# One issue line for the first loads: joint Wq/Wk quarters on SP, and eight first projections over eight PSUM banks

## The chip, the cores and the metric

The kernel runs on one core of a Trainium2 chip. The metric is the device time of one execution in microseconds (us). Engines are named as in the profile: PE (matmul), PEld (its weight loads), DVE (vector), ACT (scalar), POOL, SP (which only issues transfers). ACTq and SPq are the rows in which ACT and SP issue transfers.

## What is computed

The reference mixes two branches over x (2048 tokens of 512 values, bf16) with a gate per token:

```
g = sigmoid((x * gate_w).sum(-1))
qkv = x @ wqkv                                  # 512 x 1536: q, k, v of 32 heads with 16 values
logits[s, w] = q[s] . k[s - 2 w] / 4,  w = 0..7   # masked before the first token
a = (softmax(logits) applied to v[s - 2 w]) @ wo
b = (gelu(layernorm(x)^T @ w1 + b1) @ w2 + b2)^T
out = g * a + (1 - g) * b
```

## The kernel before

All work is registered as operations of a small planner in the kernel (`_Sched`, L48 to L271). An operation has an engine, an estimated duration, what it reads and writes, and a priority. `_pass` (L145) plays the list through with these estimates and so fixes one order for each engine; `plan_waits` (L234) then gives every instruction the semaphore waits that it needs. For a transfer, `lands` can state a due time at which the planner is to take it for finished; it changes the planned order and nothing else. Two chains written out by hand fix the order on DVE (L957) and of part of ACT.

The part that matters here is the start. Q and K are computed transposed: a projection (`f_proj`, L612) is four matmuls of 128x128 weights on 512 tokens, one for each 128 rows ("quarter", 0 to 3) of wqkv, added up in one PSUM bank. Its rhs is `XT`, x transposed. Sixteen-value heads are split over four interleaved column sets, so Q of one block of 512 tokens takes four projections (q0 to q3), and K four (k0 to k3).

For block 0, XT comes in two ways. Its quarter 0 is loaded plainly (`d_xp`, 128 columns of x for 512 tokens, rows of 256 B), transposed on PE (`f_tr`, L540, instructions on L544) and copied out of PSUM by ACT (`ev_tra`, L553) and DVE (`ev_trb`, L555). Quarters 1 to 3 are written transposed by a transposing transfer (`ld_xt0`, L470, issued on L473). Blocks 1 to 3 come by transposing transfers of all four quarters (`ld_xt`, L457, issued on L460). Plain x for the layernorm comes by `ld_x` (L439), weights by `ld_w` (L447). All plain transfers are issued on L429. PE runs matmuls on a constant (`f_warm`, L532, instructions on L536) until the first data are there.

Order of the first issues before the change:

- ACT: `d_xp` (128 KB), then quarter 0 of Wq (128 KB).
- SP: block 0's transposing transfer (384 KB), quarters 1, 2, 3 of Wq (128 KB each), quarters 0-1 and 2-3 of Wk (256 KB each), x tiles 0-1 (256 KB), block 1's transposing transfer (512 KB), x tiles 2-3, x tiles 4-7, blocks 2 and 3, x tiles 8-11 and 12-15, Wv, and then the weights of the later stages. From x tiles 2-3 on, each issue waits for an earlier transfer to have landed (`throttle`, L433: the fifth before it in `init_dmas`).

The first eight projections (L633) run in groups: q0 to q3 with quarter 0 into banks 0 to 3, then the same four with quarter 1, 2 and 3, then k0 to k3 with quarters 0-1 into banks 4 to 7, then k0 to k3 with quarters 2-3. That is 4 + 4 + 4 + 4 + 8 + 8 = 32 matmuls. ACT copies each finished bank to SBUF (L625 for Q, L628 for K and V). After them PE runs the projections of the other blocks in banks 0 to 3 (`seq_proj`, L643), first the eight of block 1.

On DVE the order from the start is: L424, `ev_trb`, layernorm statistics of x tiles 0 to 3 (`ln1`, L572), then the first two products of Q and shifted K (`qkm`, L688), which need Q and K of blocks 0 and 1. Reductions of these products on PE (`qkr`, L696) free the product buffers. Later come the softmax (L742 to L775), the weighted sum of V (L795 to L800) and the mix (`cmb`, L897). PE goes on with the first and second layer of the token branch (L810, L860) and the output projection (L876).

Of the kernel before, what the change touches and what calls it, by code (L numbers as in the profile page):

```python
# [13 lines left out]
D = 512  # L14
# [319 lines left out]
def bass_gated_mix__sliding_local_dilated__mixer_token_mlp__prompt_kernel(nc, A_x, A_wqkv, A_wo, B_x, B_w1, B_b1, B_w2, B_b2, gate_w, out, dbg=None):  # L334
    with contextlib.ExitStack() as es:
# [3 lines left out]
        sch = _Sched()  # L339

        x2d = A_x[0]
        xv = x2d.rearrange("(t p) d -> p t d", p=128)
        wqkv_v = A_wqkv.rearrange("(dt p) c -> p dt c", p=128)
# [7 lines left out]
        WQKV = view("WQKV", BF16, [(3 * D, 4), (1, 3 * D)])  # L351
# [63 lines left out]
        A = sch.add  # L415
# [12 lines left out]
        def mk_dma(dst, src):  # L428
            return lambda e: e.dma_start(dst, src)  # L429

        init_dmas = []
# [4 lines left out]
        def prev_dma():  # L436
            return [init_dmas[-1]] if init_dmas else []

        def ld_x(t0, n, q="sp"):  # L439
            ds = sch.dsem("x%d" % t0)  # L440
            op = sch.dma(q, mk_dma(X[:, t0:t0 + n, :], xv[:, t0:t0 + n, :]), n * 128 * D * 2, ds,
                         writes=["x%d" % t for t in range(t0, t0 + n)], deps=throttle() if q == "sp" else [], after=prev_dma() if q == "sp" else [], name="d_x%d" % t0)
            if q == "sp":
                init_dmas.append(op)
            return op

        def ld_w(tn, d0, n, q="sp"):  # L447
            ds = sch.dsem("wqkv%d_%d" % (tn, d0))
            op = sch.dma(q, mk_dma(WQKV[:, d0:d0 + n, tn * D:(tn + 1) * D], wqkv_v[:, d0:d0 + n, tn * D:(tn + 1) * D]),
                         n * 128 * D * 2, ds, writes=["wqkv%d_%d" % (tn, dt) for dt in range(d0, d0 + n)],  # L450
                         deps=throttle() if q == "sp" and n == 4 else [], after=prev_dma() if q == "sp" else [],
                         issue=0.65 if n == 4 else 0.45, name="d_wp%d_%d" % (tn, d0))
            if q == "sp":
                init_dmas.append(op)
            return op
# [14 lines left out]
        def ld_xt0():  # L470
            ds = sch.dsem("xt0")
            dst = XT[:, 1:4, 0:512]
            op = sch.dma("sp", lambda e: e.dma_start_transpose(dst, x2d[0:512, 128:512]), 512 * 384 * 2, ds, issue=1.25,  # L473
                         writes=XT0[1:4], after=prev_dma(), name="d_xt0")
            init_dmas.append(op)
            return op

        XP = view("OUTS", BF16, [(128, 4), (1, 128)])
        d_xp = sch.dma("act", mk_dma(XP, xv[:, 0:4, 0:128]), 512 * 128 * 2, sch.dsem("xp"), writes=["outs0"], issue=0.4, name="d_xp")

        first_loads = [ld_w(0, 0, 1, "act"), ld_xt0(), ld_w(0, 1, 1), ld_w(0, 2, 1), ld_w(0, 3, 1), ld_w(1, 0, 2), ld_w(1, 2, 2),
                       ld_x(0, 2)]
        ld_xt(1)
        first_loads.append(init_dmas[-1])
        for op_, t_ in zip(first_loads, (3.4, 4.6, 5.0, 5.4, 5.8, 6.6, 7.4, 8.2, 10.6)):
            op_.lands = t_
            op_.deps.clear()
        d_xp.lands = 3.1
        first_loads[0].order.add(d_xp)
        init_dmas[:] = [first_loads[1]] + first_loads[5:]  # L490
        ld_x(2, 2)
        ld_x(4, 4)
        ld_xt(2)
# [6 lines left out]
        def ld_w1(j):  # L500
# [4 lines left out]
            if j < 4:  # L505
# [8 lines left out]
                       writes=["wo"], deps=throttle(), after=prev_dma(), name="d_wo")  # L514
# [4 lines left out]
        for i_, (v_, n_) in enumerate(((B_b1, NFT), (B_b2, NST))):  # L519
# [6 lines left out]
          writes=["btc"], name="t_b")  # L526
# [5 lines left out]
        def f_warm(n, w_=D):  # L532
            def fn(e):
                ins = None
                for _ in range(n):
                    ins = e.matmul(ps[:, 7, 0:w_], lhsT=CONE[:, 0:128], rhs=CONE[:, 0:w_], start=True, stop=True)  # L536
                return ins
            return fn

        def f_tr(h):  # L540
# [8 lines left out]
        w2_ = A("pe", f_warm(1, 256), 0.2, writes=["lg7_0", "lg7_1"], name="warm2", prio=-100)  # L549
        ta_ = A("pe", f_tr(0), 0.215, reads=["outs0", "ident"], writes=["lg5_0", "lg5_1"], after=[w2_], name="tr0", prio=-100)  # L550
        tr_ = A("pe", f_tr(1), 0.215, reads=["outs0", "ident"], writes=["lg6_0", "lg6_1"], after=[ta_], name="tr1", prio=-100)
        w3_ = A("pe", f_warm(1), 0.43, writes=["lg7_0", "lg7_1"], after=[tr_], name="warm3", prio=-100)
        A("act", lambda e: e.activation(out=XT[:, 0, 0:256], in_=ps[:, 5, 0:256], func=AF.Copy), 0.35, reads=["lg5_0", "lg5_1"],  # L553
          writes=["xt0_0"], name="ev_tra", prio=0)
        A("dve", lambda e: e.tensor_copy(out=XT[:, 0, 256:512], in_=ps[:, 6, 0:256]), 0.35, reads=["lg6_0", "lg6_1"],  # L555
# [74 lines left out]
        tnames = ["q", "k", "v"]  # L630
        first = [(tn, dl) for tn in range(2) for dl in range(4)]
        fbn = [["acc%d" % b] for b in range(4)] + [["lg%d_0" % b, "lg%d_1" % b] for b in range(4, 8)]
        for (b0, d0, d1, s0, s1) in ((0, 0, 1, 0, 512), (0, 1, 2, 0, 512), (0, 2, 3, 0, 512), (0, 3, 4, 0, 512), (4, 0, 2, 0, 512), (4, 2, 4, 0, 512)):  # L633
            for b in range(b0, b0 + 4):
                tn, dl = first[b]
                last_main[0] = A("pe", f_proj(tn, dl, 0, b, d0, d1, s0, s1), 0.216 * (d1 - d0) * (s1 - s0) / 512,
                                 reads=xt_of(0, d0, d1) + ["wqkv%d_%d" % (tn, dt) for dt in range(d0, d1)],
                                 writes=fbn[b], after=[last_main[0]], name="pf_%s%d_%d_%d" % (tnames[tn], dl, d0, s0))
                last_main[0].order.add(w3_)
# [411 lines left out]
```

## Time and profile before

| | |
|---|---|
| time, median of 3 runs | 168.57 us (168.3 to 168.81) |
| the profiled execution: own time | 168.55 us |
| its span, first to last instruction | 167.3 us |
| PE busy | 162.1 us (97%) |
| DVE busy | 151.3 us (90%) |
| ACT busy | 75.1 us (45%) |
| granted TensorE clock, mean | 1.000 |
| transfers | 29.64 MB, mean 177 GB/s |

Starts are in us from the start of the span. A chain of waits is followed back from the last instruction: each piece is what the next one waited for. "x8" means eight instructions in one row; a row can hold many that run back to back. The profile shows a matmul of 512 columns as 379 ns long, though a new one starts every 0.2156 us when nothing is waited for, since matmuls overlap. For a transfer the profile gives when its engine issued it, how long the issue took, and how long after the start of the issue the data had landed.

### The profile page before, as it was taken

The numbers are of one execution on the slowest core, as the hardware profiler recorded it, in microseconds if no ns is written. First come the engines' busy times: TensorE is split into PE (matmuls) and PEld (weight loads), VectorE is DVE, ScalarE is ACT, GpSimd is POOL, SyncE is SP. The second block draws the span as 40 slices with busy tenths as digits, with TensorE's granted clock in tenths as the row PEclk, the third lists the DMA queues.
The fourth block names the chain that finished last, engine by engine and source line by source line (L and its number), as shares of the span: only waits on it lengthen the run. The fifth ranks groups of instructions, "written<-read, shape, count | busy, mean of one in ns | idle before, by whom it ended". The sixth has DMA issues, their size and how long they took to land.

```text
span 167.3 us, 2136 instructions
## 1 busy us (share of the span) xinstructions
PE 162.1 (97%) x845; PEld 77.5 (46%) x859; DVE 151.3 (90%) x154; ACT 75.1 (45%) x116; POOL 0.7 (0%) x8
## 2 busy tenths in 40 slices
PE   7699999999999999999999999999999999999994
PEld 2355555554454444444444444444444444444463
DVE  1055999999999999999999999999999999999896
ACT  3077688889899818793131121131231321310100
POOL 1000000000000000000000000000000000000000
PEclk9999999999999999999999999999999999999999
DMA  5999999959003846996779926462672570000454
GB/s 135 327 268 216 314 316 290 303 165 308 2 0 97 311 116 179 307 290 155 181 189 340 339 76 142 113 187 71 181 218 83 138 223 0 0 0 0 157 190 159
DMA packets 47625, 29.64 MB, mean 177 GB/s; under 512 B 9856, under 2 KB 46464, under 8 KB 47616
## 3 DMA queue, kind: packets, MB, share of 16 engines
q1 hardware_dynamic: 45120, 24.85, 54.4%
q10 hardware_dynamic: 2496, 4.66, 10.2%
q8 instruction: 7, 0.11, 0.3%
q14 instruction: 2, 0.02, 0.0%
HBM read 21.24 MB, written 2.10 MB: 140 GB/s over the span
## 4 chain that ended last, share of the span: by engine, by line
PE 91%; DMA 3%; DVE 2%; ACT 2%; issue 1%; ACTq 0%
PE ps L860 29%; PE ps L810 29%; PE ps L617 23%; PE ps L876 6%; PE ps L696 4%; DMA arena<-in_A_wqkv_dram 3%; DVE arena L897 2%; ACT L585 1%; ACT arena L628 1%; ACTq L429 0%; ACT arena L585 0%
## 5 line engine op out<-in xcount | busy, mean ns | idle before, releaser
L860 PE MATMUL ps<-arena 128*128 128x512 bf16 x220 | 48.5, 379 | 0.2
L810 PE MATMUL ps<-arena 128*128 128x512 bf16 x219 | 48.2, 379 | 0.4 <-issue 0.2
L617 PE MATMUL ps<-arena 128*128 128x512 bf16 x188 | 41.4, 379 | 1.6 <-DMA arena<-in_A_wqkv_dram 1.3
L688 DVE TENSOR_TENSOR arena<-arena 128x4096 bf16<-128x4096 bf16 (+1 forms) x12 | 35.5, 2998 | 2.5 <-ACT arena L628 2.1
L795 DVE TENSOR_TENSOR arena<-arena 128x8192 bf16<-128x8192 bf16 x8 | 35.0, 4419 | 0.0
L860 PEld LDWEIGHTS ps<-arena 128*128 128x128 bf16 x224 | 21.9, 98 | 26.4
L810 PEld LDWEIGHTS ps<-arena 128*128 128x128 bf16 x224 | 21.8, 98 | 26.6 <-ACT arena L726 0.4
L617 PEld LDWEIGHTS ps<-arena 128*128 128x128 bf16 x192 | 21.6, 113 | 21.5 <-issue 1.8
L928 ACT ACTIVATE arena<-ps,arena 128x512 bf16<-128x512 f32 x16 | 12.5, 778 | 39.4 <-PE ps L860 39.4
L798 DVE TENSOR_TENSOR arena<-arena 128x4096 bf16<-128x4096 bf16 (+1 forms) x16 | 27.0, 1751 | 0.0
L628 ACT ACTIVATE arena<-ps 128x512 bf16<-128x512 f32 x32 | 18.6, 596 | 4.5 <-PE ps L617 4.5
L831 ACT ACTIVATE arena<-ps,arena 128x512 bf16<-128x512 f32 x14 | 9.6, 687 | 22.2 <-PE ps L810 16.6
L572 DVE BATCH_NORM_STATS2 arena<-arena 128x6 f32<-128x512 bf16 x16 | 10.0, 682 | 6.1 <-DMA arena<-in_A_x_dram 6.1
L876 PE MATMUL ps<-arena 128*128 128x512 bf16 (+1 forms) x79 | 14.1, 336 | 0.1
L897 DVE SCALAR_TENSOR_TENSOR arena<-ps,arena 128x512 bf16<-128x512 f32 (+1 forms) x20 | 11.5, 637 | 0.9 <-PE ps L876 0.7
L596 ACT ACTIVATE arena<-arena 128x512 bf16<-128x512 bf16 x16 | 12.2, 804 | 0.0
L625 ACT ACTIVATE arena<-ps 128x512 bf16<-128x512 f32 x16 | 9.0, 597 | 6.2 <-PE ps L617 6.1
L876 PEld LDWEIGHTS ps<-arena 128*128 128x128 bf16 x80 | 7.8, 98 | 6.2
L672 DVE SCALAR_TENSOR_TENSOR arena<-arena 128x512 bf16<-128x512 bf16 x16 | 10.1, 689 | 0.0
L742 DVE TENSOR_TENSOR arena<-arena 128x512 bf16<-128x512 bf16 (+4 forms) x11 | 7.3, 667 | 0.6 <-ACT arena L761 0.2
L696 PE MATMUL ps<-arena 128*32 128x512 bf16 x128 | 7.3, 380 | 0.0
L726 ACT ACTIVATE arena<-ps 128x512 bf16<-128x512 f32 x8 | 4.7, 592 | 4.6 <-PE ps L696 4.6
(42 smaller groups left out, 40.0 us busy)
## 6 DMA issues: line engine op xcount, KB each, us to landing
arena<-in_B_w_dram SPq DMA_DIRECT2D x7, 1024.0 KB, 8.5
arena<-in_B_w_dram SPq DMA_DIRECT2D x8, 896.0 KB, 5.2
arena<-arena ACTq DMA_DIRECT2D x32, 128.0 KB, 2.9
arena<-in_A_x_dram SPq DMA_DIRECT2D x4, 512.0 KB, 6.1
out_dram<-arena SPq DMA_DIRECT2D x14, 128.0 KB, 1.7
arena<-in_A_x_dram SPq DMA_DIRECT2D x1, 1536.0 KB, 7.9
arena<-in_A_wqkv_dram SPq DMA_DIRECT2D x2, 256.0 KB, 3.8
arena<-in_A_x_dram SPq DMA_DIRECT2D x2, 256.0 KB, 3.6
```

The costliest lines, as they stand in the source:

```text
L596: A("act", (lambda t_: (lambda e: e.activation(out=X[:, t_, :], in_=X[:, t_, :], func=AF.Identity, scale=col(RSTD, t_), bias=col(NMR, t_)) ...
L617: ins = e.matmul(ps[:, bank, s0:s1], lhsT=lhsT, rhs=XT[:, dt, sb * 512 + s0:sb * 512 + s1], start=(dt == 0 and s0 == 0), stop=(dt == 3))
L628: return lambda e: e.activation(out=dst, in_=ps[:, bank, :], func=AF.Copy)
L688: return lambda e: e.tensor_tensor(out=PBL[buf][:, :, 512 * c0:512 * (c0 + nc_)], in0=in0, in1=in1, op=ALU.mult)
L696: ins = e.matmul(ps[32 * c:32 * c + 32, 4 + wl, :], lhsT=RP, rhs=PBL[buf][:, wl, c * 512:(c + 1) * 512], start=(dl == 0), stop=(dl == 3), ...
L795: A("dve", (lambda o_, i0, i1: (lambda e: e.tensor_tensor(out=o_, in0=i0, in1=i1, op=ALU.mult)))(pv, in0, in1), 4.4, reads=v_res + ["atx_% ...
L798: A("dve", (lambda pv_, n__: (lambda e: e.tensor_tensor(out=pv_[:, 0:n__], in0=pv_[:, 0:n__], in1=pv_[:, n__:2 * n__], op=ALU.add)))(pv, n ...
L810: ins = e.matmul(ps[:, bank, :], lhsT=W1W[:, slot, st, 128 * e_:128 * e_ + 128], rhs=X[:, st, :], start=(st == 0), stop=(st == NST - 1))
L860: ins = e.matmul(ps[:, bank, :], lhsT=W2S[slot][:, ft, 128 * e_:128 * e_ + 128], rhs=UT[:, ft, :], start=(ft == 0), stop=(ft == NFT - 1))
L876: ins = e.matmul(ps[:, bank, 0:c1 - c0], lhsT=OT[:, t, 128 * i:128 * i + 128], rhs=WO[:, t, c0:c1], start=(t == 0), stop=(t == 3))
L897: A("dve", (lambda i_, b_, c0_, c1_: (lambda e: e.scalar_tensor_tensor(out=T1[:, i_, c0_:c1_], in0=ps[:, b_, 0:c1_ - c0_], scalar=col(G, i ...
L928: A("act", (lambda i_, bank_: (lambda e: e.activation(out=T1[:, i_, :], in_=ps[:, bank_, :], func=AF.Identity, scale=col(OMG, i_), bias=co ...
```

## The change

The first loads are all issued on SP, in one line: `d_xp`, quarter 0 of Wq and Wk together (256 KB, rows of 2 KB), block 0's transposing transfer, quarters 1, 2 and 3 of Wq and Wk together (256 KB each), block 1's transposing transfer, x tiles 0-1. Then the line goes on as before. The due times for the planner are new. The first projections run in groups over all eight banks: q0 to q3 and k0 to k3 with quarter 0, the same eight with quarter 1, then q0 to q3 with quarter 2 and with quarter 3, then k0 to k3 with quarters 2-3 (8 + 8 + 4 + 4 + 8 = 32 matmuls). One more matmul on a constant, of 256 columns, stands ahead of them.

```diff
-        d_xp = sch.dma("act", mk_dma(XP, xv[:, 0:4, 0:128]), 512 * 128 * 2, sch.dsem("xp"), writes=["outs0"], issue=0.4, name="d_xp")
-
-        first_loads = [ld_w(0, 0, 1, "act"), ld_xt0(), ld_w(0, 1, 1), ld_w(0, 2, 1), ld_w(0, 3, 1), ld_w(1, 0, 2), ld_w(1, 2, 2),
-                       ld_x(0, 2)]
+        d_xp = sch.dma("sp", mk_dma(XP, xv[:, 0:4, 0:128]), 512 * 128 * 2, sch.dsem("xp"), writes=["outs0"], issue=0.4, name="d_xp")
+
+        def ld_qk(d):
+            ds = sch.dsem("wqk%d" % d)
+            op = sch.dma("sp", mk_dma(WQKV[:, d, 0:2 * D], wqkv_v[:, d, 0:2 * D]), 2 * 128 * D * 2, ds,
+                         writes=["wqkv0_%d" % d, "wqkv1_%d" % d], after=prev_dma(), issue=0.45, name="d_wqk%d" % d)
+            init_dmas.append(op)
+            return op
+
+        first_loads = [ld_qk(0), ld_xt0(), ld_qk(1), ld_qk(2), ld_qk(3)]
         ld_xt(1)
         first_loads.append(init_dmas[-1])
-        for op_, t_ in zip(first_loads, (3.4, 4.6, 5.0, 5.4, 5.8, 6.6, 7.4, 8.2, 10.6)):
+        first_loads.append(ld_x(0, 2))
+        for op_, t_ in zip(first_loads, (3.9, 5.3, 6.1, 6.8, 7.5, 9.6, 10.4)):
             op_.lands = t_
             op_.deps.clear()
         d_xp.lands = 3.1
         first_loads[0].order.add(d_xp)
-        init_dmas[:] = [first_loads[1]] + first_loads[5:]
+        init_dmas[:] = [first_loads[1]] + first_loads[3:]
...
-        w3_ = A("pe", f_warm(1), 0.43, writes=["lg7_0", "lg7_1"], after=[tr_], name="warm3", prio=-100)
+        A("pe", f_warm(1), 0.43, writes=["lg7_0", "lg7_1"], after=[tr_], name="warm3", prio=-100)
+        w3_ = A("pe", f_warm(1, 256), 0.2, writes=["lg7_0", "lg7_1"], after=[tr_], name="warm4", prio=-100)
...
-        for (b0, d0, d1, s0, s1) in ((0, 0, 1, 0, 512), (0, 1, 2, 0, 512), (0, 2, 3, 0, 512), (0, 3, 4, 0, 512), (4, 0, 2, 0, 512), (4, 2, 4, 0, 512)):
-            for b in range(b0, b0 + 4):
+        for (b0, nb, d0, d1, s0, s1) in ((0, 8, 0, 1, 0, 512), (0, 8, 1, 2, 0, 512), (0, 4, 2, 3, 0, 512), (0, 4, 3, 4, 0, 512),
+                                         (4, 4, 2, 4, 0, 512)):
+            for b in range(b0, b0 + nb):
```

In the order that the planner makes of it, PE and DVE keep their order but for these first groups. On ACT the two issues go, the copies of the first banks come in the order q0, q1, q2, k0, q3, k1, k2, q0 of block 1, k0 of block 1, k3, and a few later copies trade places with a neighbour. Block 2's transposing transfer now waits for quarter 3 of Wq/Wk, block 3's for block 1's, and x tiles 8-11 for x tiles 0-1.

## Prediction

> **What bounds the kernel now.** I read the chain of waits first, in order of time:
>
> ```profile
> 0.80 0.46 ACTq L429
> 1.25 0.03 issue
> 1.28 4.24 DMA arena<-in_A_wqkv_dram
> 5.52 0.09 issue
> 5.61 8.36 PE ps L617 x38
> ...
> 154.72 6.92 PE ps L876 x32
> 161.64 0.02 issue
> 161.67 3.98 DVE arena L897 x9
> ```
>
> The kernel waits 5.6 us for quarter 0 of Wq (issued by ACT at 1.28, landed 4.24 later); from then on PE runs to the end. Whatever moves PE's first projection moves the end, if no new wait appears. Next, the timeline of the start (start, length, engine and line):
>
> ```profile
> 0.80 1.35 SPq L473 DMA_TRANSPOSE arena<-in_A_x_dram  x1
> ...
> 2.22 2.49 SPq L429 DMA_DIRECT2D arena<-in_A_wqkv_dram  x5
> 3.30 0.34 PEld L544 LDWEIGHTS ps<-arena 128*128 128x128 bf16 x4 [0.66 <-issue]
> ...
> 3.96 0.42 DVE L555 CAST arena<-ps 128x256 bf16<-128x256 f32 x1 [2.45 <-PE ps L544]
> 4.75 0.47 SPq L429 DMA_DIRECT2D arena<-in_A_x_dram  x1
> 5.27 3.36 SPq L460 DMA_TRANSPOSE arena<-in_A_x_dram  x1
> 5.58 14.39 PEld L617 LDWEIGHTS ps<-arena 128*128 128x128 bf16 x68 [1.82 <-issue]
> 5.61 14.62 PE L617 MATMUL ps<-arena 128*128 128x512 bf16 x66 [1.26 <-DMA arena<-in_A_wqkv_dram]
> ```
>
> XT's quarter 0 is ready at 4.38, when the cast on L555 ends. PE has nothing to do until 5.61, and then starts a matmul every 0.2156 us. Last, the transfers in half microseconds (last two columns: busy share, GB/s):
>
> ```profile
> 2.00:2.50 0.50, 0.50 (x2) 0.15 (x1) 0.00 (x0) 0.50 (x1) 0.00 (x0) 1.00 0.67 153
> 2.50:3.00 0.50, 0.50 (x3) 0.15 (x1) 0.00 (x0) 0.50 (x1) 0.00 (x0) 1.00 1.28 287
> ...
> 5.50:6.00 0.50, 0.39 (x2) 0.26 (x3) 0.00 (x0) 0.00 (x0) 0.00 (x0) 1.00 1.00 316
> ...
> 8.00:8.50 0.50, 0.50 (x4) 0.29 (x3) 0.00 (x0) 0.00 (x0) 0.00 (x0) 1.00 1.62 231
> ```
>
> From 2 us on they are never idle: order, not latency, decides when a byte arrives.
>
> **The change, part by part.** Sizes in thousands of bytes: d_xp 131, a single Wq quarter 131, a joint quarter 262, block 0's transposing transfer 393, block 1's 524.
>
> *Start of the first group.* It needs the joint quarter 0 and XT's quarter 0. SP issues d_xp at 0.80 (0.46 long, as ACT's row) and the joint quarter at 1.28; the transposing transfer now comes behind it. Data flow from about 2.0; 393 have moved by about 3.6 by the windows (77 by 2.5, 220 by 3.0, 364 by 3.5), and the distance from moved to landed is 0.9 to 1.0 below: 4.5. So the group starts at 4.5 in place of 5.61, and 8 matmuls take 1.72: to 6.2. A start up to 0.4 later costs nothing, as the next wait is later. The added 256-column matmul (its twin before the data took 0.42) ends before 4.5: nothing.
>
> *Second group: the new limit.* It needs quarters 1 of XT and of the weights. By the line, 131+262+393+262 = 1048 must have moved. Before the change exactly as much had to be moved for Wq's quarter 3 (131+131+393+3x131), issued at 3.29 and landed 3.3 later, at 6.6. Summing the windows, 1048 are moved at 5.66, so 0.94 passes from moved to landed. A second way: transposing alone ran slower than the rest (about 520 of block 1 between 8.0 and 10.2: 245 GB/s, where plain loads ran at 316 to 354). Then 2.1 + 131 at 220 GB/s + 262 at 340 + 393 at 245 + 262 at 340 ends at 5.84, landing 6.8. The bounds from rows of issue to landing: issue of quarter 1 at 3.25 (0.80 + 0.46 + 0.5 + 1.35 and gaps), plus 3.3, the shortest of the wqkv rows, is 6.55; plus 4.2, the longest, is 7.45. I take 6.7.
>
> *The rest of the first 32.* 24 matmuls follow without a break: 6.7 + 24 x 0.2156 = 11.87. Before: 5.61 + 32 x 0.2156 = 12.51. Gain 0.64. Quarter 2 is due at 8.42 and quarter 3 at 9.29; as many bytes (1310 and 1573, the two Wk transfers) had landed before at 7.45 and 8.2 (issue 3.75 and 4.24, plus 3.7 and 4.0), so both are in time.
>
> *Block 1 and x tiles 0-1 change places.* Block 1, at 2097 bytes of the line, lies between x tiles 0-1 (1835, landed 4.1 after 4.75: 8.85) and its old place (2359, landed 5.5 after 5.27: 10.8): about 9.9, needed at 11.87. SP issues it at about 4.7 and, by the 3.36 row, is held by it to about 8, so x tiles 0-1 are issued at 8.0 and land at about 11 (the transfer that followed block 1 before took 3.0), x tiles 2-3 at 11.7 as before. The four statistics on DVE (1.29 for two) then end at about 13.5 in place of 13.02. The products they precede wait for K of block 1 anyway: 15.07 before, 2.56 after the first 32 matmuls, so 14.43 now. Nothing lost; the cover ends if x tiles 2-3 land 0.9 later than that.
>
> *Behind it.* Blocks 2 and 3 were issued at 9.81 and 13.62 and land at 15.8 and 18.3; they are needed 8 and 9 projections (0.8624 each) after the first 32: 18.8 and 19.6. Their changed waits point at transfers landed by 10. ACT loses two issues and has the same copies; copied banks are reused 3.4 us later, and a copy takes 0.60. DVE is dense too (90%), but at 42.15 it waits for PE's reductions, and these start on PE 1.2 after DVE's last product (37.36 to 38.58); near the end it waits again 0.72 for the output projection. So up to about 1.2 of PE's gain passes through.
>
> *Sum.* The profiled execution took 168.55 (span 167.3 and 1.25 around it), practically the median 168.57. 168.55 - 0.64 = **167.9**.
>
> *A rule against it.* In the first half microsecond of transfers, with d_xp and the transposing transfer flowing, only 153 GB/s were moved. The Trainium skill ("DMA: Bandwidth & Descriptors", Specifications) asks for at least 512 B per piece for line rate; d_xp has rows of 256 B, and now all the rest queues behind it. The traces before, with two queues, can't show that alone. What it would do is the second rival.
>
> **The rivals.**
>
> *No second wait* (gain 1.1): the transposing transfer and quarter 1 are there by 6.2. Then 4.5 + 32 x 0.2156 = 11.4, 167.4. For: landing of quarter 1 was 0.3 behind the transposing transfer's (6.0 and 5.7). Against: 1048 bytes by 5.3 means 320 GB/s from the first moment, and the first windows show 153 and 287.
>
> *d_xp holds the line.* Before, its slow pieces ran beside another queue's; now nothing runs beside them. If its 131 flow at the 153 of the first window (0.86) in place of 220 (0.60), and the transposing transfer starts late by as much again, everything behind is 0.4 later: second group at 7.1, end at 12.27, gain 0.24, 168.3. The rule above names this.
>
> *The transposing transfer takes its time from its issue: slower.* It landed 4.9, 5.5, 6.0 and 4.7 after issue in the four cases seen. It is now issued at 1.83 in place of 0.80. If 5.5 to 6.0 hold, it lands at 7.3 to 7.8 and quarter 1 0.3 behind: second group at about 7.9, end 13.07, 169.1. The price begins where the second group starts after 12.51 - 24 x 0.2156 = 7.34. For: the issue moves back a full microsecond, and it no longer runs beside another queue, where the busy share was 1.27. Against: the 5.5 and 6.0 were behind about 900 of other bytes; 393 stand ahead here, mostly gone at 3.2.
>
> *Gained, then lost:* x tiles 2-3 or block 3 slip by over a microsecond (SP held longer by block 1) and PE waits there: about 168.5.
>
> **How the numbers follow.** Forecast (second group between 6.3 and 7.0) 0.50; no second wait 0.12; d_xp 0.15; transposing transfer late 0.15; lost later 0.08. A measurement can tell about 0.3%, 0.5 us. Faster by more than that needs the second group before 6.85: most of the forecast, 0.38, and the 0.12: 0.50. Slower: the late transposing transfer, beyond its threshold by enough, 0.13. The same: 0.37. The range goes from the second case (167.4, less 0.1 for the spread of runs) to between the bound of 7.45 (168.66) and the slower rival: 167.3 to 168.9.
>
> **What would show it.** The first projection matmul at about 4.5, eight of them, a wait for quarter 1 ending near 6.7, the first product on DVE at about 14.4, and PE's reductions at 37.9. If the wait names the transposing transfer and ends after 7.34, the slower rival holds; if L544's matmuls start after 3.5, d_xp does. If PE shows a wait near 12, 18.8 or 19.6, or DVE's statistics end after 14.4, the gain is lost there. The forecast is wrong if the start is right and the reductions aren't earlier.

## Result and profile after

The changed kernel takes 168.97 us (median of 20 runs) where the kernel before takes 168.38 beside it (20 runs; the 168.57 of the first table was of three). The ratio of the two is 1.0037, with a 95% interval of 1.0019 to 1.0055: slower, by 0.3 to 0.9 us. The forecast was 167.9, a gain. A second set of runs of the same kernel (after_again below) gives a ratio of 0.9997 [0.996, 1.0034], which tells no difference; its medians, 168.9 against 168.5, point the same way. About one execution in four of the kernel before, and of the experiments that keep two queues, takes 169.7 us or more, and two of the changed kernel's 20 took 351.94, which no run here explains and the ratio leaves out; two of the profiles below are of such long executions, and it is said there.

The chain of waits of the changed kernel, in order of time (start, length, what):

```profile
4.50 0.08 issue
4.58 2.70 PE ps L625 x8
7.28 0.06 issue
7.34 6.42 PE ps L625 x29
...
154.72 6.92 PE ps L885 x32
```

The first group starts at 4.58, a microsecond earlier than the 5.61 of the page before. But its eight matmuls take until 7.28, and the second group starts at 7.34. The profile names no wait between them, since the modelled ends reach over it; by the starts the second group could have followed at 7.1. From there on all is as it was: the last 32 matmuls of the output projection start at 154.72 in both pages. 7.34 + 24 x 0.2156 = 12.51 is the end of issue of the first 32 matmuls, the same 12.51 as 5.61 + 32 x 0.2156. The text below calls this moment **T32**.

The timeline of the start (start, length, engine and line, operation; in brackets the idle time before it and what ended it):

```profile
1.84 1.50 SPq L473 DMA_TRANSPOSE arena<-in_A_x_dram  x1
...
3.38 1.51 SPq L429 DMA_DIRECT2D arena<-in_A_wqkv_dram  x3
...
4.58 25.59 PE L625 MATMUL ps<-arena 128*128 128x512 bf16 x111
...
11.25 2.47 DVE L580 BATCH_NORM_STATS2 arena<-arena 128x6 f32<-128x512 bf16 x4 [6.93 <-DMA arena<-in_A_x_dram]
...
15.07 4.50 DVE L697 TENSOR_TENSOR arena<-arena 128x4096 bf16<-128x4096 bf16 x2 [1.36 <-ACT arena L636]
```

SP issues the joint quarter 1 only at 3.38, when the issue of the transposing transfer is over, and the list of transfers has it landed 3.8 later, at 7.2 (the last number, counted from the start of its issue):

```profile
arena<-in_A_wqkv_dram SPq DMA_DIRECT2D x1, 256.0 KB, 3.8
```

The second group starts 0.14 after that landing. The statistics on DVE and the first product (15.07, as before) stand 2.56 behind T32, as was worked out. The transfers of the same kernel in half microseconds (last three columns: clock, busy share, GB/s):

```profile
2.00:2.50 0.50, 0.50 (x3) 0.15 (x2) 0.00 (x0) 0.08 (x1) 0.00 (x0) 1.00 0.88 200
2.50:3.00 0.50, 0.50 (x3) 0.14 (x1) 0.00 (x0) 0.00 (x0) 0.00 (x0) 1.00 1.13 178
3.00:3.50 0.50, 0.50 (x5) 0.26 (x4) 0.00 (x0) 0.00 (x0) 0.00 (x0) 1.00 0.73 279
...
2.00:5.50 3.50, 3.42 (x13) 1.26 (x12) 0.42 (x1) 0.47 (x2) 0.00 (x0) 1.00 1.10 252
```

And the whole stretch from 2.0 to 5.5 in the kernel before:

```profile
2.00:5.50 3.50, 2.35 (x9) 0.75 (x7) 0.42 (x1) 1.51 (x2) 0.00 (x0) 1.00 1.13 285
```

252 GB/s against 285: in the one line, 889 thousand bytes have moved by 5.5, where 997 had before. The bytes ahead of quarter 1 come later than the old curve says, on which the forecast rested: summed over the windows, 1048 thousand have moved at 6.07, not at 5.66.

### The profile page after: what moved, and what is told of

Its sections match the earlier page's. It is cut to its first block, busy times and chain, and to the rows that moved or that the text cites. A ratio compares the mean times of both kernels' runs of the same rounds, so it can differ in the third digit from the quotient of the medians.

```text
span 167.3 us, 2136 instructions
## 1 busy us (share of the span) xinstructions
PE 163.2 (98%) x846; PEld 77.7 (46%) x860; DVE 151.2 (90%) x154; ACT 74.8 (45%) x116; POOL 0.7 (0%) x8
## 4 chain that ended last, share of the span: by engine, by line
PE 95%; DVE 2%; issue 1%
PE ps L869 29%; PE ps L819 29%; PE ps L625 25%; PE ps L885 6%; PE ps L705 4%; DVE arena L906 2%; PE ps L543 2%; PE ps L551 0%
## 5 line engine op out<-in xcount | busy, mean ns | idle before, releaser
L937 ACT ACTIVATE arena<-ps,arena 128x512 bf16<-128x512 f32 x16 | 12.5, 778 | 39.4 <-PE ps L869 39.4
L636 ACT ACTIVATE arena<-ps 128x512 bf16<-128x512 f32 x32 | 18.8, 599 | 3.5 <-PE ps L625 3.4
L885 PE MATMUL ps<-arena 128*128 128x512 bf16 (+1 forms) x79 | 14.1, 336 | 0.1
L633 ACT ACTIVATE arena<-ps 128x512 bf16<-128x512 f32 x16 | 9.3, 602 | 7.9 <-PE ps L625 7.9
L735 ACT ACTIVATE arena<-ps 128x512 bf16<-128x512 f32 x8 | 4.7, 592 | 4.6 <-PE ps L705 4.6
```

The source lines that it names most:

```text
L636: return lambda e: e.activation(out=dst, in_=ps[:, bank, :], func=AF.Copy)
L885: ins = e.matmul(ps[:, bank, 0:c1 - c0], lhsT=OT[:, t, 128 * i:128 * i + 128], rhs=WO[:, t, c0:c1], start=(t == 0), stop=(t == 3))
L937: A("act", (lambda i_, bank_: (lambda e: e.activation(out=T1[:, i_, :], in_=ps[:, bank_, :], func=AF.Identity, scale=col(OMG, i_), bias=co ...
```

## Experiments

Six theories, under the names that the expectations use. LINE: T32 is set by the landing of quarter 1, for which the second group waits, and passes on to the end one to one. Why that landing is late: BYTES (1048 thousand bytes stand ahead of and in it, in any queue), ALONE (a transposing transfer is slower than its bytes when nothing runs beside it), HOLE (the transfers pause where the line passes from plain to transposing), QUEUES (one queue moves less than two). CLOCK is the rival that needs no transfer: PE's first matmuls run at half rate, and their number sets T32.

The table has every run beside those of the kernel before that shared its chip. "Quarter 1" is the landing of the last data that the second group needs, GB/s is that of 2.0 to 5.5. Columns 4 to 7 are of one profiled execution, its own time in column 3.

| kernel | median; ratio [95%] | profiled | first group | quarter 1 | T32 | GB/s |
|---|---|---|---|---|---|---|
| before, first page | 168.57 | 168.55 | 5.61 | 6.0 | 12.51 | 285 |
| after | 168.97; 1.0037 [1.0019, 1.0055] | 168.62 | 4.58 | 7.2 | 12.51 | 252 |
| before_again | 168.09; 0.9974 [0.9939, 1.001] | 167.83 | 4.55 | 5.6 | 11.81 | 298 |
| after_again | 168.9; 0.9997 [0.996, 1.0034] | 169.15 | 4.56 | 7.8 | 13.13 | 235 |
| old_groups | 170.01; 1.0107 [1.0062, 1.0151] | 169.49 | 4.56 | 7.3 | 13.47 | 246 |
| xp_on_act | 169.59; 1.0079 [1.0041, 1.0118] | 169.23 | 5.41 | 7.2 | 13.2 | 262 |
| joint_old_queues | 168.78; 1.0024 [0.9979, 1.0069] | 170.14 | 5.17 | 6.3 | 14.1 | 278 |
| plain_xt0 | 168.48; 1.0011 [0.9974, 1.0048] | 168.22 | 4.43 | 6.9 | 12.20 | 268 |
| line_old_quarters | 169.13; 1.0051 [1.0031, 1.007] | 169.34 | 4.37 | 6.6 | 13.21 | 206 |
| swap_only | 168.19; 1.001 [0.9975, 1.0046] | 168.74 | 4.78 | in time | 12.29 | 287 |
| q1_ahead | 168.52; 1.0017 [0.999, 1.0044] | 168.53 | 4.72 | 6.9 | 12.35 | 246 |
| transposer_first | 171.5; 1.0187 [1.0131, 1.0242] | 171.58 | 7.42 | 7.5 | 15.5 | 217 |
| bridge | 168.02; 0.9985 [0.9954, 1.0016] | 167.98 | 5.00 | in time | 11.9 | 295 |
| transposer_on_act | 168.64; 0.9994 [0.9947, 1.0042] | 168.33 | 4.91 | 6.3 | 12.32 | 294 |
| joint_old_bridge | 168.16; 0.9955 [0.9912, 0.9998] | 170.95 | 6.11 | 6.7 | 14.9 | 290 |
| k0_on_act | 168.75; 0.999 [0.994, 1.004] | 167.67 | 4.63 | 5.8 | 11.6 | 298 |

The medians of the kernel before beside these runs were 168.5 (before_again to xp_on_act), 168.15 (joint_old_queues to swap_only), 168.25 (q1_ahead to bridge) and 168.52 (the last three). In q1_ahead quarter 1 itself landed at 5.37 and the second group needs the transposing transfer, landed at 6.89. In every profile but two the span is T32 + 154.8; there it is 0.15 and 0.4 more (q1_ahead, swap_only). That alone bears out the second half of LINE: in the other fourteen nothing behind the first 32 matmuls took the difference back or added to it.

### before_again, after_again: both kernels profiled once more

No edit.

> The kernel before, profiled once more. Its profiled execution in the shown profile took 168.55 while its fastest runs take 167.7. Theory LINE (what decides is when the loads of the second group land): the first projection starts where quarter 0 of Wq lands, and a faster execution than the one shown has it earlier than 5.52, by as much as the execution is faster, with all matmuls of the first 32 at 0.216 us. Theory CLOCK (what decides is when PE goes from one matmul per 0.43 us to one per 0.216): the landing is near 5.5 again, and the difference between executions is the number of projection matmuls that still run at 0.43.

> The changed kernel, profiled once more. LINE: the second group starts at 7.2 to 7.5 whatever the first group does, because the joint quarter 1 lands at about 7.2 behind the transposing transfer. CLOCK: the first group is still running when quarter 1 lands, since more than four of its matmuls take 0.43, and the second group starts later than 7.4 with no wait for a transfer.

The chain of waits of the kernel before in its second profile:

```profile
0.80 1.36 SPq L473
...
2.21 3.42 DMA arena<-in_A_wqkv_dram
5.63 0.14 issue
5.77 7.50 PE ps L617 x34
```

That of the changed kernel in its second:

```profile
1.84 1.82 SPq L473
...
3.70 4.12 DMA arena<-in_A_wqkv_dram
7.82 0.14 issue
7.96 6.43 PE ps L625 x29
```

Both begin with the issue of the transposing transfer (L473), behind which quarter 1 is issued, and both end in a wait for it. The kernel before is here not held by quarter 0, which landed at 4.46 and not at 5.52, but by quarter 1 of Wq: 5.77 + 28 x 0.2156 = 11.81, and 167.83 us. So the 5.61 of the first page was one execution's. The changed kernel waits 1.50 for quarter 1 here, by the waits of PE. Against this page of the kernel before, quarter 1 comes 1.6 to 2.2 later and pays back four more matmuls in the first group, 4 x 0.2156 = 0.86: T32 moves by +0.7 to +1.3. LINE's number for the second group, 7.2 to 7.5, was missed by 0.5, but the wait that it names is there; CLOCK is not what stopped it, since the first eight matmuls were over by 6.3.

### old_groups: the changed loads, the old order of matmuls

```diff
-        for (b0, nb, d0, d1, s0, s1) in ((0, 8, 0, 1, 0, 512), (0, 8, 1, 2, 0, 512), (0, 4, 2, 3, 0, 512), (0, 4, 3, 4, 0, 512),
-                                         (4, 4, 2, 4, 0, 512)):
+        for (b0, nb, d0, d1, s0, s1) in ((0, 4, 0, 1, 0, 512), (0, 4, 1, 2, 0, 512), (0, 4, 2, 3, 0, 512), (0, 4, 3, 4, 0, 512),
+                                         (4, 4, 0, 2, 0, 512), (4, 4, 2, 4, 0, 512)):
```

> The changed loads with the old groups of matmuls (q with quarter 0, 1, 2, 3, then k). LINE: the first group of four is done by 6.3, PE waits for quarter 1 until 7.3 with 28 matmuls to go in place of 24, so the first 32 end 4 x 0.2156 = 0.86 later than in the changed kernel: about 169.7. CLOCK: the four matmuls that are moved behind the wait run at 0.216 in place of 0.43, the loss is smaller: 169.0 to 169.3.

Slower than the changed kernel, 170.01 in the median. Quarter 1 landed at 7.29, and 28 matmuls instead of 24 were left: 7.43 + 28 x 0.2156 = 13.47, which is T32. The eight banks are worth their four matmuls, and the loads alone cost more than the whole change does.

### xp_on_act: the plain columns back in ACT's queue

```diff
-        d_xp = sch.dma("sp", mk_dma(XP, xv[:, 0:4, 0:128]), ...
+        d_xp = sch.dma("act", mk_dma(XP, xv[:, 0:4, 0:128]), ...
```

> The changed kernel with the plain columns of x issued by ACT again; the rest of the line starts 0.5 earlier on SP. LINE: block 0's transposing transfer and the joint quarter 1 land up to 0.5 earlier, the second group starts at 6.8 to 7.0, and the time falls by 0.3 to 0.5 against the changed kernel. CLOCK: the first group is as slow as before, and nothing is gained.

A gain of 0.3 to 0.5 was expected and a loss came. The chain of waits:

```profile
0.81 3.36 DMA arena<-in_A_x_dram
...
4.30 0.59 PE ps L551 x4
```

In a queue of their own the plain columns landed 3.36 after issue, at 4.17, where in the changed kernel PE transposes them from 3.27 on. The joint quarter 0 was issued in the same moment on SP. (In the kernel before, the transposing transfer beside them took 1.35 to issue, and they landed after 2.3 to 2.4.) The first group moved to 5.41, its matmuls ran at half rate until 7.4, and T32 came to 13.2. So the second rival of the prediction (d_xp holds the line) is wrong: at the head of the one line the plain columns are quick, landed 2.2 to 2.3 after issue, and with them out of that line quarter 1 landed no earlier (7.2).

### joint_old_queues: joint quarters and eight banks, the two queues of before

```diff
+        d_xp = sch.dma("act", ...
+        first_loads = [ld_qk(0, "act"), ld_xt0(), ld_qk(1), ld_qk(2), ld_qk(3)]
```

> The changed kernel with the plain columns and the joint quarter 0 issued by ACT and the transposing transfer first on SP, as before; joint quarters and eight banks stay. ALONE: the transposing transfer lands at 5 to 5.7 again, quarter 1 at about 6.3; the first group starts at 5 to 5.8 with the joint quarter 0 and the second needs no wait; the first 32 end at 12.0 to 12.7: about the time before, 0.5 better than the changed kernel. BYTES: quarter 1 lands at 7.0 or later as in the changed kernel, and the time is that of the changed kernel.

Quarter 1 landed at 6.3, 0.9 to 1.5 before the changed kernel's, with the same 1048 thousand bytes ahead of and in it: against BYTES. It is the landing that ALONE had given. SP issued it at 2.22, where the changed kernel did at 3.38 and 3.70. PE did not wait for it. The profiled execution (170.14) is one of those near 170, and what made it long is in its groups of matmuls from 5 to 9.3 (count, busy time, mean ns of one, idle before):

```profile
L626 PE MATMUL ps<-arena 128*128 128x512 bf16 x10 | 4.4, 620 | 0.7 <-DMA arena<-in_A_wqkv_dram 0.7
```

Ten matmuls in 4.4 us: one every 0.43, half the usual rate, until 9.36.

### plain_xt0: a plain transfer in place of block 0's transposing one

```diff
-            e.dma_start_transpose(dst, x2d[0:512, 128:512])
+            mk_dma(dst, x2d[0:384, :].rearrange("(q p) d -> p q d", p=128))
```

> The changed kernel with block 0's transposing transfer replaced by a plain one of the same bytes at the same place of the line (the quarters 1 to 3 of block 0 then hold x untransposed, so those projections work on other values). Theory ALONE (the transposing transfer costs the line more than its bytes: it keeps SP 1.5 to 1.8 us and moves slowly when no other queue runs beside it): quarter 1 lands at about 6.3 in place of 7.2 to 7.8, no wait of more than 0.3 before the second group, the time falls by 0.6 to 1.3 against the changed kernel, to about 167.8. Theory BYTES (262 thousand bytes more stand ahead of the second group than before, whatever they are): quarter 1 lands at 7.0 or later, and the time falls by less than 0.3.

The chain of waits:

```profile
2.30 4.59 DMA arena<-in_A_wqkv_dram
...
7.03 6.42 PE ps L625 x29
```

Quarter 1 could be issued at 2.30 in place of 3.38, since a plain issue is short, and landed at 6.89: 0.3 to 0.9 earlier than with the transposing transfer, and not at the 6.3 of ALONE. The median, 168.48, is 0.4 to 0.5 below the changed kernel's, between what the two theories said. The transposing transfer explains a part; how much, one landing does not tell. The trace keeps 16 marks for each transfer, as many as the core has DMA engines, and the landing is the last of them: here 15 had come by 6.36 and the 16th at 6.89, while in joint_old_queues all 16 came by 6.35. The rates are close too, 268 GB/s in the plain line and 278 in the two queues of joint_old_queues:

```profile
2.00:5.50 3.50, 3.31 (x15) 1.45 (x14) 0.42 (x1) 0.47 (x2) 0.00 (x0) 1.00 0.95 268
...
2.00:5.50 3.50, 2.84 (x11) 1.00 (x10) 0.42 (x1) 1.50 (x2) 0.00 (x0) 1.00 1.12 278
```

So without the transposing transfer one line came close to two queues, but for one late part.

### line_old_quarters: the kernel before, with ACT's two loads at the head of SP's line

```diff
-        d_xp = sch.dma("act", ...
+        d_xp = sch.dma("sp", ...
-        first_loads = [ld_w(0, 0, 1, "act"), ld_xt0(), ...
+        first_loads = [ld_w(0, 0, 1), ld_xt0(), ...
```

> The kernel before with the two issues of ACT moved to the head of SP's line and nothing else (single quarters, old groups). ALONE: the transposing transfer lands at about 5.9 as in the changed kernel, Wq's quarter 1 at 6.6 to 7.0, the 28 matmuls that follow end at 12.7 to 13.1 in place of 11.8 to 12.5 before: slower by 0.6 to 0.9, as much as the whole change or more. BYTES: with 786 thousand bytes ahead as before, Wq's quarter 1 lands at 5.6 to 6.0 as before, and the time is the same as before.

The transfers from 2.0 to 5.5 of this kernel (last column GB/s):

```profile
2.00:5.50 3.50, 3.39 (x13) 1.16 (x11) 0.42 (x1) 0.46 (x2) 0.00 (x0) 1.00 0.94 206
```

And its chain of waits where it passes the last of the Wk quarters 0-1:

```profile
5.05 4.66 DMA arena<-in_A_wqkv_dram
...
9.76 4.94 PE ps L617 x22
```

Moving these two loads alone, with the old quarters and groups, makes the kernel slower by about as much as the whole change (1.0051): 206 GB/s, quarter 1 of Wq at 6.6 instead of 5.6 to 6.0 with no more bytes ahead of it, and a later wait until 9.76 for quarters 0-1 of Wk, landed at 9.71, which had landed at 7.45 on the first page. This is the second run against BYTES. ALONE had given these landings (6.6 to 7.0 for quarter 1), and QUEUES fits as well. The edit moves more than a queue: with two loads issued ahead on SP, the transposing transfer is issued at 1.84 in place of 0.80, and quarter 1 of Wq at 3.50 in place of 2.2. From its issue it took 3.09, less than the 3.4 to 3.8 before, so its lateness here is that of its issue. Of the 16 marks of Wk's quarters 0-1, 12 had come by 8.08.

### swap_only: only block 1 ahead of x tiles 0-1

```diff
-        first_loads = [ld_w(0, 0, 1, "act"), ..., ld_w(1, 2, 2), ld_x(0, 2)]
+        first_loads = [ld_w(0, 0, 1, "act"), ..., ld_w(1, 2, 2)]
         ld_xt(1)
         first_loads.append(init_dmas[-1])
+        first_loads.append(ld_x(0, 2))
```

> The kernel before with x tiles 0-1 issued behind block 1's transposing transfer, as in the change, and nothing else. Both theories: PE's first 32 matmuls are as before; the statistics on DVE start at about 11 in place of 8.9 and end before the first product, the time is the same within 0.3. If this part costs, DVE's first product starts later than 2.6 after the end of the first 32.

No difference in time (1.001). But the chain of waits of its profile runs through block 3:

```profile
10.81 5.25 SPq L460
...
16.10 4.25 DMA arena<-in_A_x_dram
...
20.48 1.91 PE ps L617 x8
```

Block 2's issue held SP for 5.25, so block 3 was issued at 16.10, landed at 20.35, and PE waited 0.24 for it. The margin that the forecast gave blocks 2 and 3 is used up by this part. In the changed kernel block 3 landed at 19.4 and no wait is seen.

### q1_ahead: the joint quarter 1 ahead of the transposing transfer

```diff
-        first_loads = [ld_qk(0), ld_xt0(), ld_qk(1), ld_qk(2), ld_qk(3)]
+        first_loads = [ld_qk(0), ld_qk(1), ld_xt0(), ld_qk(2), ld_qk(3)]
```

> The changed kernel with the joint quarter 1 issued ahead of block 0's transposing transfer. The same 1048 thousand bytes must land for the second group, only the order of the last two differs. Theory HOLE (the transposing transfer brings its first data 1.2 to 1.5 us after its issue, and in the changed kernel the line is empty before that, at 3 to 3.5; and SP can issue nothing while it issues that transfer): quarter 1 fills the hole, the transposing transfer is issued at 2.35 and lands about 4.1 later, at 6.4; the second group starts at about 6.5 with no or a short wait, the first 32 end at 11.5 to 11.8, and the time falls by 0.8 to 1.2 against the changed kernel, to 167.7 to 168.0. Theory BYTES (only the number of bytes ahead counts): the second group starts at 7.2 to 7.8 as in the changed kernel, and the time doesn't change.

The last of the second group's data, now the transposing transfer, landed at 6.89. The second group started at 7.18, straight behind a first group with four matmuls at half rate, and the median came 0.4 below the changed kernel's, not 0.8 to 1.2: one line moves 246 GB/s in either order. HOLE falls in the form that it had, that the order inside the line decides. The pause that it names is in the traces all the same: 82 GB/s from 2.8 to 3.1 in the changed kernel, 77 from 2.7 to 3.1 in after_again and 38 from 3.1 to 3.4 in line_old_quarters, against 285 to 291 from 2.8 to 3.1 in before, joint_old_queues and transposer_on_act, and 341 in plain_xt0. It is not the whole loss: by 3.5 the changed kernel is 30 thousand bytes behind the kernel before, by 5.5 108.

### transposer_first: the transposing transfer at the head of the one line

```diff
-        first_loads = [ld_qk(0), ld_xt0(), ld_qk(1), ld_qk(2), ld_qk(3)]
+        first_loads = [ld_xt0(), ld_qk(0), ld_qk(1), ld_qk(2), ld_qk(3)]
```

> The changed kernel with block 0's transposing transfer at the head of SP's line and the plain columns and the joint quarters behind it: one line still, the same bytes ahead of the second group. HOLE: no hole at 3 to 3.5, the transposing transfer lands at 5 and quarter 1 at 6.3 to 6.6, a microsecond earlier than in the changed kernel; but the plain columns and quarter 0 are late now (plain columns at 4.5 to 5), the first group starts at 5.5 to 6 and the first 32 end at 12.4 to 12.9 with no wait behind the first group: about the time of the changed kernel. BYTES: quarter 1 lands at 7.2 to 7.8, and there is a wait for it.

The chain of waits:

```profile
0.80 1.34 SPq L473
...
2.19 3.98 DMA arena<-in_A_x_dram
6.18 0.14 issue
6.31 0.59 PE ps L552 x4
```

Far slower (1.0187). The plain columns, second in the line, landed 3.98 after their issue at 2.19, though only 393 thousand bytes stood ahead. 4.5 to 5 was expected for them, and 6.3 to 6.6 for quarter 1, which came at 7.52. So behind the transposing transfer the plain columns are slow too, and this order costs their whole delay: the first group starts at 7.42.

### bridge: the kernel before, with two more constant matmuls

```diff
-        w3_ = A("pe", f_warm(1), 0.43, ..., name="warm3", prio=-100)
+        w3_ = A("pe", f_warm(3), 1.29, ..., name="warm3", prio=-100)
```

> The kernel before with two more matmuls on a constant behind the transposes, so that PE has no gap between 4.0 and the first projection; nothing else. Theory CLOCK (the change from one matmul per 0.43 to one per 0.216 us comes after a stretch of unbroken work that starts over when PE pauses, so that in some executions the first 20 matmuls run at the slow rate): the executions near 170, about a quarter of those before, get rarer, and the median falls by 0.2 to 0.5. If the moment doesn't depend on the pause, the executions near 170 stay as frequent, and the median stays within 0.2 of the one before.

168.02 against 168.25, a ratio of 0.9985 [0.9954, 1.0016]: no difference that can be told. None of its 12 runs took 169.7 us or more, where 3 of the 23 of the kernel before beside it did; that fits CLOCK's reading, that a pause of PE ahead of the first projection keeps it at half rate longer, and is too few to show it.

### transposer_on_act: the changed kernel, with block 0's transposing transfer alone in ACT's queue

```diff
-            op = sch.dma("sp", lambda e: e.dma_start_transpose(dst, x2d[0:512, 128:512]), ...
+            op = sch.dma("act", lambda e: e.dma_start_transpose(dst, x2d[0:512, 128:512]), ...
...
+        first_loads[5].deps.add(first_loads[1])
```

(the added line makes block 1's transfer wait for block 0's).

> The changed kernel with block 0's transposing transfer issued by ACT at the start, so that it has a queue of its own, and all else in the one line of SP (block 1's transposing transfer now waits until block 0's has landed). Theory QUEUES (what the change lost is the second queue: a transposing transfer and plain loads in one line move 208 to 254 GB/s between 2.0 and 5.5, side by side in two queues 280 to 301): the 1048 thousand bytes have moved by 5.6 to 5.8 in place of 6.1 to 6.4, the second group starts at 6.3 to 6.8 in place of 7.3 to 8.0, and the time falls by 0.6 to 1.0 against the changed kernel, to 167.9 to 168.3. Theory HOLE (only the place of the transposing transfer inside the line): the same gain, as there is nothing ahead of it; but the rate between 2.0 and 5.5 stays below 270 GB/s. BYTES: second group at 7.2 or later, no gain.

The transfers, to be read against the same rows of the changed kernel above:

```profile
2.50:3.00 0.50, 0.50 (x3) 0.15 (x1) 0.00 (x0) 0.50 (x1) 0.00 (x0) 1.00 1.28 287
3.00:3.50 0.50, 0.50 (x5) 0.22 (x4) 0.00 (x0) 0.50 (x1) 0.00 (x0) 1.00 1.22 321
...
2.00:5.50 3.50, 3.13 (x12) 1.16 (x11) 0.42 (x1) 1.67 (x2) 0.00 (x0) 1.00 1.10 294
```

From the chain of waits, the first projections:

```profile
4.91 10.17 PE ps L625 x44
```

The same bytes in two queues: 287 and 321 GB/s where one line moved 178 and 279, 294 in place of 252 over the stretch, and quarter 1 at 6.3 in place of 7.2 to 7.8. From 4.91 on PE is never stopped. QUEUES had forecast this. BYTES is out, and so is HOLE, which kept the rate below 270. ALONE is not: here too the transposing transfer runs beside another queue. Part of the gain is plain: SP can issue quarter 1 at 1.83, as the transposing issue no longer holds it until 3.38. Whether that is all is open. plain_xt0 has the short issue too, in one line, with 268 GB/s and 6.9; but 15 of the 16 marks of its quarter 1 had come by 6.36, against 6.18 here.

The time gained less than the landing: 168.64, 0.3 below the changed kernel, and the intervals of the two ratios overlap. Five of its 12 runs took 169.7 or more. Three to four of the first matmuls ran at half rate, and the first group starts at 4.91: 4.91 + 32 x 0.2156 is 11.81, which is the T32 of before_again. Even without the wait, the joint quarters and eight banks have nothing over the kernel before when that one is not disturbed.

### joint_old_bridge: joint_old_queues with two full constant matmuls in place of the short one

```diff
-        w3_ = A("pe", f_warm(1, 256), 0.2, ..., name="warm4", prio=-100)
+        w3_ = A("pe", f_warm(2), 0.86, ..., name="warm4", prio=-100)
```

> The kernel with joint quarters and eight banks on the old two queues, with three matmuls on a constant of 512 columns in place of one of 512 and one of 256 ahead of the projections, so that PE has no pause while it waits for the joint quarter 0. CLOCK: the executions near 170 and above, four of ten without it, go; the median falls from 168.78 to 168.2 to 168.4. If the moment of the faster rate doesn't depend on the pause, they stay, and the median with them.

168.16 against 168.52, 0.9955 [0.9912, 0.9998]: the only kernel whose interval lies below 1, by a hair, and one of 15 such intervals can do that by chance. The median is where CLOCK had it, but two of the 12 runs still took over 170.7, which by CLOCK should have gone. Its profiled execution (170.95) is of the long kind, and its chain of waits shows what these look like:

```profile
5.11 1.00 issue
6.11 8.97 PE ps L626 x32
```

Quarter 0 came late (15 of its 16 marks by 4.91, the last at 6.02), PE paused 1.00 in spite of the added matmuls, and ran at half rate until about 9.9.

### k0_on_act: the kernel before, with quarter 0 of Wk third in ACT's queue, its four matmuls in the first group, and one more constant matmul

```diff
+        d_k0 = ld_w(1, 0, 1, "act")
...
-        for (b0, d0, d1, s0, s1) in ((0, 0, 1, 0, 512), (0, 1, 2, 0, 512), ..., (4, 0, 2, 0, 512), (4, 2, 4, 0, 512)):
+        for (b0, d0, d1, s0, s1) in ((0, 0, 1, 0, 512), (4, 0, 1, 0, 512), (0, 1, 2, 0, 512), ..., (4, 1, 2, 0, 512), (4, 2, 4, 0, 512)):
```

> The kernel before with quarter 0 of Wk split off and issued third by ACT, the four K matmuls of quarter 0 in banks 4 to 7 right behind the four of Q, and one more matmul on a constant ahead. QUEUES: two queues stay, 131 thousand bytes more stand ahead of Wq's quarter 1, which lands at 5.9 to 6.3, and PE has eight matmuls to fill that time from 4.6 to 6.3: first 32 done at 11.5 to 11.8 in place of 11.8 to 12.5, time 0 to 0.4 below the one before. If quarter 0 of Wk lands later than 5.5, PE waits in the middle, and nothing is gained.

The best profiled execution of all, 167.67: first group at 4.63, 0.1 of waiting behind it, T32 11.6, 0.2 before before_again's. The runs do not bear it out: 168.75 in the median, 0.999 [0.994, 1.004], with 5 of 12 at 169.7 or more. So eight first matmuls over eight banks, without joint quarters and without one line, gain nothing that can be told either.

## Why the prediction was wrong

**Right.** The first group at 4.5 (4.58, and 4.56 the second time). Quarters 2 and 3 in time (7.8 and 8.5), block 1 too (10.4 against a need at 12.5). X tiles 0-1 at about 11 (11.25), their statistics harmless, and the first product 2.56 behind T32. What T32 gains or loses reaches the end: of 16 profiles two differ from this by more than 0.1. Blocks 2 and 3 were in time, though closer than said.

**The step that failed: "Second group: the new limit".** The step counted the bytes of the line correctly and took their landing, 6.6, from the curve of the kernel before, or 6.8 from its rates; 6.7 was used. It was 7.2 and 7.8. That curve was one of two queues side by side: 278 to 298 GB/s in the eight profiles in which ACT's queue carries a quarter or the transposing transfer, 262 where it carries the plain columns alone. One line with the transposing transfer moved 206 to 252, and one line without it 268. Quarter 1 was issued at 3.38 and 3.70, not 3.25, since the issue of the transposing transfer took 1.50 and 1.82 (1.35 before), and landed 3.8 and 4.1 later, not 3.3. The upper bound of 7.45 did not hold the second profile: it had the issue as fixed. The prediction named 7.34 as the start at which the gain is gone; the first profile stands on it, the second 0.6 beyond.

Both terms of the step's sum were too small. The 1048 thousand bytes were moved at 6.07 and 6.42, not at 5.66, and the distance from moved to landed was 1.13 and 1.40, not 0.94. That distance, read off one landing, is no constant, because the last of the 16 marks makes the landing. For quarter 1 (of Wq alone in before and before_again):

| kernel | issued | 12th mark | 15th | last |
|---|---|---|---|---|
| before | 2.22 | 5.51 | 5.96 | 5.98 |
| before_again | 2.21 | 5.34 | 5.37 | 5.63 |
| after | 3.38 | 6.58 | 7.04 | 7.20 |
| after_again | 3.70 | 7.10 | 7.36 | 7.82 |
| plain_xt0 | 2.30 | 6.21 | 6.36 | 6.89 |
| joint_old_queues | 2.22 | 6.30 | 6.33 | 6.35 |
| transposer_on_act | 1.83 | 6.16 | 6.18 | 6.33 |

In the first profile most of quarter 1 was there before 6.7, and the wait was for the rest. No run here shows which part is late, or why.

**The slower rival had the right side and the wrong carrier.** It had the second group at 7.9 because the transposing transfer would be late. That one landed 4.1 after its issue, at 5.9, in both profiles. Quarter 1 behind it was late.

**The base was one execution's.** The gain of the first group, 5.61 to 4.5, was worked out against a page in which quarter 0 landed at 5.52. Twelve of its 16 marks had come by 4.51 there, the last four from 5.38 on. In before_again all had come by 4.46, and quarter 1 was the limit. Most of the microsecond that the step counted was thus not there to be had: the right sum is the later landing of quarter 1 (1.6 to 2.2) less four matmuls (0.86), +0.7 to +1.3 against that page. The medians differ by 0.6, and the lowest runs (167.68 before, 168.47 after) by 0.8.

**Not seen at all: the rate of the first matmuls.** The step let the first group take 8 x 0.2156 = 1.72. In the first profile it took longer, as the weight loads in the timeline of the changed kernel show, one ahead of each matmul (start, length; in brackets the idle time before):

```profile
4.96 0.15 PEld L625 LDWEIGHTS ps<-arena 128*128 128x128 bf16 x1 [0.27 <-issue]
5.39 0.15 PEld L625 LDWEIGHTS ps<-arena 128*128 128x128 bf16 x1 [0.28 <-issue]
5.82 0.15 PEld L625 LDWEIGHTS ps<-arena 128*128 128x128 bf16 x1 [0.28 <-issue]
6.24 0.55 PEld L625 LDWEIGHTS ps<-arena 128*128 128x128 bf16 x3 [0.28 <-issue]
```

The loads from 4.96 to 6.24 come every 0.43, those after it three in 0.55: four matmuls cost 0.8 too much. Here the wait for quarter 1 covers it, as after_again shows: there all eight ran at 0.216 and T32 was later still. But with quarter 1 at 6.7 in the first profile the second group would have started at 7.1 all the same, and T32 been 12.3: 0.2 gained and not 0.64. In transposer_on_act and q1_ahead, where quarter 1 came sooner, it was the next limit.

Left open: why the line was late. That one line with the transposing transfer in it moves less than two queues is shown: 206 to 252 GB/s in six profiles, 278 to 298 in eight. Three readings of it are left. One queue may move less than two (QUEUES). The transposing transfer may move less with nothing beside it, and pause before its first data (ALONE, and the pause of HOLE). Or its long issue is what costs: from issue to landing quarter 1 took 3.8 and 4.1 in the changed kernel, no longer than the 4.1 of joint_old_queues and the 4.5 of transposer_on_act, but it was issued 1.2 to 1.9 later. plain_xt0 takes both the transposing and its issue out of the line, and in its rate and in 15 of the 16 marks of quarter 1 comes nearer to the two queues than to the changed kernel, which speaks for the last two, though its landing, 6.9, does not; its plain transfer is another pattern of bytes than the transposing one, and no run has the same plain loads in one queue and in two. The Trainium skill ("DMA: Bandwidth & Descriptors", Issuing engines are not separate DMA queues) says that issuing from several engines saves only the issuers' time. These rows show that this time matters (1.50 to 1.82 here, no small part of 7); whether it is the only saving they do not settle. Open as well is what decides when PE's rate doubles.

## What to carry to other kernels

Do not read a landing off a curve of bytes moved if the change merges the queues that made the curve; measure or bound the rate of the merged line by itself, and count a long issue in it as time in which the next transfer does not exist. Do not take the distance from moved to landed from one row: the last part decides, and it can come most of a microsecond after the others. Profile the kernel before twice before working out a gain at its start: which of two waits holds it may change from one execution to the next, and the gain is against the later limit. Where a group of matmuls is moved ahead, check the rate at which PE runs at that moment.

## What the runs showed of the hardware

- A transposing transfer holds the engine that issues it: 384 KB for 1.34 to 2.51 us, 512 KB for 1.9 to 5.3. It is longer behind other transfers (2.51 in q1_ahead, fourth in the line, against 1.34 at its head).
- Where a queue passes to a transposing transfer, the rate can fall almost to nothing. The half microseconds of swap_only between 8.0 and 9.0, while SP is still issuing block 1's (4.76 to 9.12; last column GB/s):

```profile
8.00:8.50 0.50, 0.50 (x4) 0.30 (x3) 0.00 (x0) 0.10 (x1) 0.00 (x0) 1.00 0.97 64
8.50:9.00 0.50, 0.50 (x4) 0.26 (x3) 0.00 (x0) 0.50 (x2) 0.00 (x0) 1.00 0.21 25
```

- A transfer is there with the last of its 16 marks. For quarter 1 of the kernels here that was 0.04 to 0.9 us after the 12th; for quarter 0 in joint_old_bridge it was 1.1 after the 15th.
- Loads of 128 KB with rows of 256 B landed 2.2 to 2.4 us after their issue at the head of a line, 3.36 beside a quarter that was issued in the same moment (xp_on_act), and 3.98 behind the transposing transfer (transposer_first).
- Matmuls of 512 columns start 0.427 apart at first and 0.2156 later, while the column of the granted clock reads 1.00 all along. The moment of the change was before 4.6 (before_again, after_again), near 6.2 (after), 7.2 (xp_on_act) and 9.3 to 9.9 (joint_old_queues, joint_old_bridge, transposer_first), though PE had run matmuls since 0.83 in all. The Trainium skill ("TensorE: Matmul & The Clock Gate", Part 1: The HAM clock gate) puts the change after about 3.4 us of sustained work and says that the moment differs from run to run. The spread here agrees with the second: the same changed kernel has the change near 6.2 in one execution and before 4.6 in the other. In the three latest PE had paused, for 0.66 and 1.00 ahead of the first projection and in transposer_first for 2.97 ahead of the transposes, but no run here separates pause and cause.
